# Block-local attention ahead of two routed expert layers: a narrower mask, block maxima taken in another order, nine tiles transposed by a DMA queue, and a new table of priorities

## The chip, the cores and the metric

The kernel runs on one core of one Trainium2 chip. The metric is the device time of one execution in microseconds (us). The engines are named as the profile names them: PE (TensorE; PEld is its weight load), DVE (VectorE), ACT (ScalarE), POOL (GpSimd) and SP (the engine that only issues DMAs here).

## What is computed

The reference is an attention over 4 batches of 8 heads, 768 positions of 64 elements, followed by two expert layers over the 3072 resulting rows. Only the attention, and the gate scores of the first expert layer that close it, are touched by the change.

```python
block, window = (32, 16)
k_sum = k.reshape(B, H, nb, block, D).max(axis=3)
v_sum = v.reshape(B, H, nb, block, D).mean(axis=3)
scores_l = scale * np.matmul(q, k.transpose(0, 1, 3, 2))
mask_l = np.abs(pos[:, None] - pos[None, :]) < window
scores_s = scale * np.einsum('bhsd,bhnd->bhsn', q, k_sum)
scores_s = scores_s + np.log(block)
scores_l_m = np.where(mask_l, scores_l, -1000000000.0)
scores_all = np.concatenate([scores_l_m, scores_s], axis=-1)
a = np.exp(scores_all - np.max(scores_all, axis=-1, keepdims=True))
a = a / (np.sum(a, axis=-1, keepdims=True) + 1e-09)
return np.matmul(a, np.concatenate([v, v_sum], axis=2))
...
logits = x @ w_gate
```

Each query sees the keys less than 16 positions away, and one summary key for each of 24 blocks of 32 positions: the elementwise maximum of the block's keys. The first expert layer then assigns all 3072 rows to 8 experts of 384 places by sorted scores, so nothing of it can begin before the last row's scores are there.

## The kernel before

**Tiling.** The attention works on 8 groups, a batch and 4 heads each (`d['n']` 0 to 7; two groups make a batch). A group is prepared by `prep` and then computed in 6 units of 128 queries (`unit`, c = 0 to 5). Positions are laid out so that one partition holds two neighbouring positions, r = 0 and 1. Numbers are carried as a float16 high part and a float16 low part (the rest), so most steps stand twice.

**Preparation of a group.** `split_qk` makes high and low parts of k and q in three chunks (ACT line 175; the subtraction at line 168 on POOL, for group 0 on DVE). `tr_k` and `tr_q` transpose them on PE (lines 192, 202, 213) into PSUM, and DVE (line 183) and ACT (line 184) copy them out. `kmax` makes the summary keys: PE transposes the float32 keys, 4 heads in each of 3 chunks (line 225, 12 matmuls), DVE reduces each chunk to maxima over 16 columns (line 227), ACT and DVE split the result (lines 229, 230), PE brings the two halves of the partitions together with a constant matrix (line 235), DVE takes the larger (lines 238, 239), and ACT and DVE split again into `ksT` (lines 240, 241). `values` splits v, sums it over blocks on PE, and lays it out in the tile `W` by 13 DMAs (lines 257, 269).

**A unit.** PE writes the mask into a PSUM bank by a matmul with an identity (line 293, 4 x 120 columns: for each head 96 local columns and 24 summary columns), adds the summary scores (line 296) and the local scores (line 302). DVE takes the row maximum (line 308), ACT the exponential (line 312), PE transposes the result (line 317), ACT and DVE split it (lines 320, 321), PE multiplies it with `W` into `po` (line 332), DVE divides (lines 334 to 336) into `xt`. After a batch's second group the rows of a unit are complete: one of 24 tiles `ti`. ACT and POOL split it into `xs` (lines 340, 341), SP writes it to the scratch tensor `xscr` (line 342), PE transposes it in 8 matmuls (line 345), ACT and DVE copy 4 of them each into `xT` (lines 184 and 183), PE computes the gate scores (lines 384, 385), ACT and DVE add them up into `L` (lines 351, 352).

**What sets the order.** Each operation is recorded with an engine, a planned duration, the tiles that it reads and writes and a priority. `Sched.order` replays them: every engine takes, among the operations whose inputs are ready in that replay, the one with the smallest priority, and each engine's instructions are then emitted in that order and run in it on the chip, whatever the real durations are. The priority is the group's and unit's number plus an entry of the table `BIAS1`, looked up by engine and tile name (a `p` ahead of the name is group 0's preparation, a `z` the last group's units). The constants of the routing stages are recorded with priority 60 through a helper whose line is 395. The expert stages have a planner of their own, with a table `BIAS2`, and follow the attention in every engine's stream.

**Buffers that matter.** The tiles `xs` exist 4 times, `xT`, `kn`, `ksT` and `W` twice. All DMAs of the attention are issued by SP, in one order; an SP instruction that waits holds all behind it.

Of the kernel before, what the change touches and what calls it, by code (L numbers as in the profile page):

```python
# [133 lines left out]
class Att:  # L134
# [51 lines left out]
    def tr_k(self, d, c, i, eng, P):  # L186
        nc=self.nc; s=d['ksp',c]; kT=d['kT']; rd=[s.name+'l',s.name+'h']
        if i==0:
            ms,tp=self.half()
            def f():  # L190
                for h in range(4):
                    for r in range(2): nc.tensor.transpose(tp[:,h,r],s[:,h,r].rearrange("p a d -> p (a d)"),self.C['idh'])
            self.pe(.45,rd,[ms.name],f,P)
            self.evac(eng,kT[:,i,:,:,8+128*c:136+128*c],tp,[ms.name],[(kT.name,i,c)],P)
            return
# [10 lines left out]
    def tr_q(self, d, c, eng, P):  # L206
# [7 lines left out]
        self.pe(.45,[s.name+'l',s.name+'h'],[ms.name],f,P)  # L214
        self.evac(eng,qT[:,:,256*c:256*c+256],tp.rearrange("p h r j -> p h (r j)"),[ms.name],[(qT.name,c)],P)

    def kmax(self, d, P):

        nc=self.nc; t=self.wk.tile; kn=d['kn']; V=nc.vector
        kp=t([128,4,24],F32,"kp"); ph,pl=t([128,96],F16,"kph"),t([128,96],F16,"kpl"); km=t([128,96],F32,"km"); ksT=d['ksT']=t([128,2,4,24],F16,"ksT")  # L220

        for c in range(3):
            ms=self.ps.tile([128,512],F32,"ms"); m3=ms.rearrange("p (h j) -> p h j",h=4)
            def f(c=c,m3=m3):
                for h in range(4): nc.tensor.transpose(m3[:,h],kn[:,c,h].rearrange("p r d -> p (r d)"),self.C['idf'])
            self.pe(.47,[(kn.name,c)],[ms.name],f,P)
            self.dve(512,[ms.name],[(kp.name,c)],lambda c=c,m3=m3: V.reduce_max(kp[:,:,8*c:8*c+8],m3.rearrange("p h (n j) -> p h n j",j=16),axis=AX.X),P)
        kk=[(kp.name,c) for c in range(3)]; kf=kp.rearrange("p h n -> p (h n)")
        self.act(96,kk,[ph.name],lambda: nc.scalar.activation(ph,kf,AF.Copy),P)
        self.dve(96,kk+[ph.name],[pl.name],lambda: V.tensor_sub(pl,kf,ph),P)  # L230

        ms=self.ps.tile([128,512],F32,"ms")
        def f():
            for r in range(2):
                for i,x in enumerate((ph,pl)): nc.tensor.matmul(ms[:,96*r:96*r+96],self.C['dup'][:,r],x,start=(i==0),stop=(i==1),skip_group_check=True)
        self.pe(.2,[ph.name,pl.name],[ms.name],f,P)
        o=[ksT[:,i].rearrange("p h n -> p (h n)") for i in range(2)]
        self.dve(96,[ms.name],[km.name],lambda: V.tensor_copy(km,ms[:,:96]),P)
        self.dve(96,[ms.name,km.name],[km.name],lambda: V.tensor_max(km,ms[:,96:192],km),P)
        self.act(96,[km.name],[(ksT.name,0)],lambda: nc.scalar.activation(o[0],km,AF.Copy),P)  # L240
        self.dve(96,[km.name,(ksT.name,0)],[ksT.name],lambda: V.tensor_sub(o[1],km,o[0]),P)

    def values(self, d, P):
# [9 lines left out]
        for i in (0,1,2,3,4,7):  # L253

            lo,hi,j,c0,c1,w=(max(0,32*i-8),min(128,32*i+40),max(0,8-32*i),0,3,slice(i,12,4)) if i<4 else (120,128,0,0,2,slice(4,12,4)) if i==4 else (0,8,40,1,3,slice(3,8,4))
            for r in range(2):
                self.dma((hi-lo)*(c1-c0)*1660,vk+['kpads'],([('We',n,r,i)] if i>3 else [])+[(W.name,r,i)],lambda lo=lo,hi=hi,p=48*r+j,c0=c0,c1=c1,w=w,r=r: nc.sync.dma_start(W[p:p+hi-lo,w],vs[lo:hi,c0:c1,r]),P)
# [11 lines left out]
        self.dma(478000,[vw.name+'h',vw.name+'l'],[(W.name,2)],lambda: nc.sync.dma_start(W[96:120],vw[:,None,:].to_broadcast([24,12,516])),P)  # L269
# [16 lines left out]
    def unit(self, d, c, T):  # L286
# [5 lines left out]
        def f():  # L292
            nc.tensor.matmul(sc,C['idb'],m[:,None,:].to_broadcast([128,4,120]),start=True,stop=False,skip_group_check=True)
# [11 lines left out]
        self.pe(.95,rd,[sn],f,T)  # L305
# [31 lines left out]
        if g==1:  # L337
# [5 lines left out]
            ms,_=self.half(); x8=ms.bitcast(F16).rearrange("p (i j) -> p i j",i=8)  # L343
            def f4():
                for i in range(8): nc.tensor.transpose(x8[:,i],xf[:,128*i:128*i+128],C['idh'])
            self.pe(.45,[xs.name+'h',xs.name+'l'],[ms.name],f4,T)
            self.evac('A',xT[:,:4],x8[:,:4],[ms.name],[xT.name+'h'],T,512)
            self.evac('D',xT[:,4:],x8[:,4:],[ms.name],[xT.name+'l'],T,512)
# [550 lines left out]
class Moe2(Ops):  # L899
# [73 lines left out]
BIAS1={'ACT L': 15.48, 'ACT a': 648.82, 'ACT ah': -1.09, 'ACT kT': -68.21, 'ACT kph': 36.51, 'ACT ksT': 18.87, 'ACT ksp': -8.93, 'ACT pkT': -5.63,   # L973
    'ACT pkph': -46.46, 'ACT pksT': 31.69, 'ACT pksp': 1.25, 'ACT pqsp': 43.19, 'ACT pvm': 72.68, 'ACT pvs': 9.61, 'ACT qsp': 11.16, 
    'ACT vm': -120.37, 'ACT vs': 49.68, 'ACT xT': 81.6, 'ACT xs': -53.13, 'ACT zL': 19.69, 'ACT za': -25.1, 'ACT zah': -84.77, 'ACT zxs': -41.97, 
    'DVE L': -4.27, 'DVE al': 631.85, 'DVE kT': -2.83, 'DVE km': 3.54, 'DVE kp': -22.03, 'DVE kpl': -22.43, 'DVE ksT': -0.4, 'DVE nb': 2.43, 
    'DVE need': -71.59, 'DVE pkT': -3.3, 'DVE pkm': 1.04, 'DVE pkp': -53.59, 'DVE pkpl': 4.91, 'DVE pksT': 33.61, 'DVE pksp': -14.27, 
    'DVE pqT': 120.54, 'DVE pqsp': -12.12, 'DVE pvs': -74.64, 'DVE qT': -80.69, 'DVE rc': -61.0, 'DVE rs': 0.4, 'DVE sc': 150.33, 
    'DVE xT': -19.42, 'DVE xt': 157.4, 'DVE zL': 73.4, 'DVE zcmp': -4.41, 'DVE zm': 31.67, 'DVE znb': -223.07, 'DVE zoh': 2.32, 
# [107 lines left out]
```

## Time and profile before

| | us |
|---|---|
| runs shown (3) | 820.58, 824.24, 826.77; median 824.24 |
| the profiled execution | 827.03 |
| its span, first to last instruction | 825.3 |

The profile's busy times are, of the span: PE 708.4 us (86%), DVE 631.1 (76%), ACT 411.8 (50%), POOL 225.9 (27%). In the trace a time such as 198.33 is counted from the span's start. The attention takes the first 228 us of the span or so; the routing of the first expert follows at once. An operation's duration in a row of the trace runs until its end is reported, so the durations of neighbours on one engine overlap a little: DVE's row maximum lasts 0.66 us, and the next instruction can start 0.57 us after it.

### The profile page before, as it was taken

What the parts mean: (1) busy time and instruction counts of PE and PEld (TensorE: products, weight loads), DVE (VectorE), ACT (ScalarE), POOL (GpSimd) and SP (SyncE); (2) the same over time, 40 slices, a digit from 0 to 9 for tenths busy, and PEclk for the clock granted to TensorE, in tenths of its full rate; (3) what the DMA queues carried; (4) which work ended last, traced back from release to release, by engine and by line L of the source; (5) the groups of instructions that cost most, each with busy time, mean ns of one, the idle gap of its engine ahead of it and who ended that gap; (6) DMA issues with size and microseconds to landing.
All of it is one profiled execution on the core that took longest, in us unless ns stands there. A gap on an engine that the chain in (4) does not pass through costs nothing. (4 is left out here: it accounts for less than half of the span.)

```text
span 825.3 us, 22067 instructions
## 1 busy us (share of the span) xinstructions
PE 708.4 (86%) x8531; PEld 483.7 (59%) x8531; DVE 631.1 (76%) x1900; ACT 411.8 (50%) x794; POOL 225.9 (27%) x233
## 2 busy tenths in 40 slices
PE   3879899898834988999989899699899998999793
PEld 2768778787633545554545454355567657775671
DVE  7999789788777788989889888666469675755750
ACT  3778889685702352525252526443444454646330
POOL 2775664631301011111111113011112222221210
PEclk9999999899955998999999999999999999999897
DMA  7686886432206095869786969999996898799810
GB/s 221 172 224 178 250 214 192 116 96 73 79 13 230 2 275 114 248 146 308 124 282 135 292 157 302 259 278 341 243 260 115 308 361 214 253 327 278 284 31 6
DMA packets 163171, 165.03 MB, mean 200 GB/s; under 512 B 75734, under 2 KB 123862, under 8 KB 163057
## 3 DMA queue, kind: packets, MB, share of 16 engines
q1 hardware_dynamic: 155184, 141.47, 62.0%
q0 software_dynamic: 7872, 22.05, 8.2%
q8 instruction: 69, 1.13, 0.6%
q14 instruction: 46, 0.37, 0.1%
HBM read 114.35 MB, written 29.91 MB: 175 GB/s over the span
## 5 line engine op out<-in xcount | busy, mean ns | idle before, releaser
L708 PE MATMUL ph<-xT,w1h 128*128 128x384 f16 x512 | 102.3, 339 | 12.7 <-DVE hl L712 7.0
L951 PE MATMUL ph<-xT,w1h 128*128 128x128 f16 x1152 | 90.7, 223 | 11.5 <-DVE hl L955 7.4
L951 PEld LDWEIGHTS <-w1h 128*128 128x128 f16 x1152 | 73.6, 100 | 16.1 <-issue 12.4
L722 PE MATMUL py<-w2h,hh 128*128 128x512 f16 x192 | 74.0, 385 | 5.6 <-ACT yt L726 5.6
L684 POOL DMA_INDIRECT xg<-xscr,idx x24 | 30.6, 1273 | 168.6 <-DVE idx L607 64.9
L708 PEld LDWEIGHTS <-w1h 128*128 128x128 f16 x512 | 47.8, 101 | 46.5 <-issue 20.4
L711 ACT ACTIVATE hh<-ph 128x384 f16<-128x384 f32 x64 | 31.3, 489 | 85.9 <-PE ph L708 71.0
L722 PE MATMUL py<-w2l,hh 128*128 128x512 f16 x192 | 74.0, 385 | 0.0
L722 PE MATMUL py<-w2h,hl 128*128 128x512 f16 x192 | 73.8, 384 | 0.0
L645 POOL DMA_INDIRECT out<-xg,oid x18 | 30.4, 1691 | 128.9 <-DVE xg L966 74.2
L925 DVE SCALAR_TENSOR_TENSOR w1l<-wst,w1h 128x1024 f16<-128x1024 f32 x44 | 52.1, 1221 | 10.2 <-ACT w1h L924 9.2
L672 ACT ACTIVATE w1h<-wst 128x1024 f16<-128x1024 f32 x32 | 33.5, 1054 | 51.0 <-DMA wst<-moe_w 50.9
L954 ACT ACTIVATE hh<-ph 128x512 f16<-128x512 f32 x36 | 21.4, 593 | 74.5 <-PE ph L951 71.9
L951 PE MATMUL ph<-xT,w1l 128*128 128x128 f16 x576 | 57.3, 223 | 0.1
L925 DVE SCALAR_TENSOR_TENSOR w2l<-wst,w2h 128x1024 f16<-128x1024 f32 x44 | 52.8, 1220 | 5.5 <-ACT w2h L924 3.7
L962 PE MATMUL py<-w2h,hl 128*128 128x512 f16 x144 | 54.6, 379 | 2.6 <-DVE hl L955 2.5
L645 POOL DMA_INDIRECT out<-yt,dni x24 | 28.0, 1167 | 104.1 <-DVE dw L757 63.4
L722 PEld LDWEIGHTS <-hh 128*128 128x128 f16 x384 | 33.8, 101 | 37.1 <-issue 8.8
L312 ACT ACTIVATE a<-sc,nb 128x120 f32<-128x120 f32 x192 | 53.8, 377 | 3.4 <-DVE nb L310 3.3
L962 PE MATMUL py<-w2h,hh 128*128 128x512 f16 x144 | 54.6, 379 | 0.0
L962 PE MATMUL py<-w2l,hh 128*128 128x512 f16 x144 | 54.6, 379 | 0.0
L924 ACT ACTIVATE w2h<-wst 128x1024 f16<-128x1024 f32 x44 | 45.6, 1052 | 17.4 <-DMA wst<-moe_w 7.1
(348 smaller groups left out, 1845.6 us busy)
## 6 DMA issues: line engine op xcount, KB each, us to landing
wst<-moe_w SPq DMA_DIRECT2D x152, 512.0 KB
ysc<-yt SPq DMA_DIRECT2D x8, 1539.0 KB
kn<-k SPq DMA_DIRECT2D x24, 256.0 KB
qn<-q SPq DMA_DIRECT2D x24, 256.0 KB
vn<-v SPq DMA_DIRECT2D x24, 256.0 KB
xscr<-xs SPq DMA_DIRECT2D x24, 256.0 KB
W<-vs SPq DMA_DIRECT2D x32, 145.1 KB
W<-vs SPq DMA_DIRECT2D x32, 120.9 KB
```

What stands on the lines that cost most here:

```text
L312: for h in range(4): nc.scalar.activation(a[:,h],sc[:,h],AF.Exp,bias=nb[:,h:h+1],scale=0.125)
L645: s=self.nc.gpsimd.indirect_dma_start(out=self.out,out_offset=bass.IndirectOffsetOnAxis(ap=idx,axis=0),in_=x,in_offset=None,bounds_check=3 ...
L672: self.act(1080,[st.name],[hk],lambda st=st,h=h: nc.scalar.activation(h,st,AF.Copy,scale=32.),P)
L684: self.s.op('POOL',1.1,[idx.name]+[('xscr',c) for c in range(24)],[xg.name],lambda xb=xb,i=i: nc.gpsimd.indirect_dma_start(out=xb,out_offs ...
L708: nc.tensor.matmul(ph[:,:384],a[:,kc,fs],b[:,kc],start=(n==0),stop=(n==11))
L711: self.act(384,[ph.name],[(hh.name,fb)],lambda ph=ph,fb=fb: nc.scalar.activation(hh[:,fb],ph[:,:384],AF.Relu),P+.1)
L722: nc.tensor.matmul(py,a[:,fb,sl],b[:,fb],start=(n==0),stop=(n==23))
L924: self.act(1080,[st.name],[hk],lambda st=st,h=h: nc.scalar.activation(h,st,AF.Copy,scale=16.),P-.2)
L925: self.dve(1024,[st.name,hk],[lk,(lk,0),(lk,1)],lambda st=st,h=h,l=l: V.scalar_tensor_tensor(l,st,16.,h,op0=ALU.mult,op1=ALU.subtract),P-.2)
L951: nc.tensor.matmul(ph[:,128*fi:128*fi+128],w[:,kc,fs],x[:,kc],start=(n==0),stop=(n==11)); n+=1
L954: self.act(512,[ph.name],[(hk,q)]+before(H,q),lambda p4=p4,o=o: nc.scalar.activation(o,p4,AF.Relu),P)
L962: nc.tensor.matmul(py,x[:,fb],w[:,fb],start=(n==0),stop=(n==23))
```

## The change

The mask's matmul covers the 96 local columns of each head alone. In `kmax` DVE first takes the larger of the two neighbouring positions for all three chunks in one instruction (`kx`, 128 x 768 float32, both inputs in SBUF), PE transposes half as many columns (6 matmuls in two PSUM tiles), DVE reduces them in two instructions, ACT and DVE split 48 columns, four matmuls with the constant matrix fill 192 columns, and one DVE copy makes `ksT`. Tiles 12 to 20 are no longer transposed by PE: SP issues a DMA transpose from `xs` to `xT`, which also takes their two copies from ACT and DVE. Some planned durations are changed, and the table `BIAS1` is replaced.

```diff
-        kp=t([128,4,24],F32,"kp"); ph,pl=...; km=t([128,96],F32,"km"); ksT=...
-        for c in range(3):
-            ms=self.ps.tile([128,512],F32,"ms"); m3=ms.rearrange("p (h j) -> p h j",h=4)
-            def f(c=c,m3=m3):
-                for h in range(4): nc.tensor.transpose(m3[:,h],kn[:,c,h].rearrange("p r d -> p (r d)"),self.C['idf'])
-            self.pe(.47,[(kn.name,c)],[ms.name],f,P)
-            self.dve(512,[ms.name],[(kp.name,c)],lambda c=c,m3=m3: V.reduce_max(kp[:,:,8*c:8*c+8],...),P)
...
-        self.dve(96,[ms.name],[km.name],lambda: V.tensor_copy(km,ms[:,:96]),P)
-        self.dve(96,[ms.name,km.name],[km.name],lambda: V.tensor_max(km,ms[:,96:192],km),P)
-        self.act(96,[km.name],[(ksT.name,0)],lambda: nc.scalar.activation(o[0],km,AF.Copy),P)
-        self.dve(96,[km.name,(ksT.name,0)],[ksT.name],lambda: V.tensor_sub(o[1],km,o[0]),P)
+        kx=t([128,3,4,64],F32,"kx",bufs=1); km=t([128,2,24],F32,"km"); kh,kl=t([128,48],F16,"kmh"),t([128,48],F16,"kml"); ksT=...
+        self.dve(1150,[(kn.name,c) for c in range(3)],[kx.name],lambda: V.tensor_max(kx,kn[:,:,:,0],kn[:,:,:,1]),P)
+        for g in range(2):
+            ms=self.ps.tile([128,512],F32,"ms")
+            def f(g=g,ms=ms):
+                for c in range(3): nc.tensor.transpose(ms[:,128*c:128*c+128],kx[:,c,2*g:2*g+2].rearrange("p h d -> p (h d)"),self.C['idf'])
+            self.pe(.4,[kx.name],[ms.name],f,P)
+            self.dve(384,[ms.name],[(km.name,g)],lambda g=g,ms=ms: V.reduce_max(km[:,g],ms[:,:384].rearrange("p (n j) -> p n j",j=16),axis=AX.X),P)
+        self.act(60,kk,[kh.name],lambda: nc.scalar.activation(kh,kf,AF.Copy),P)
+        self.dve(500,kk+[kh.name],[kl.name],lambda: V.tensor_sub(kl,kf,kh),P)
...
+                for e in range(2): nc.tensor.matmul(m4[:,i,:,e],self.C['dup'][:,e],x.rearrange("p (g n) -> p g n",g=2),start=True,stop=True,skip_group_check=True)
+        self.dve(192,[ms.name],[ksT.name],lambda: V.tensor_copy(ksT.rearrange("p i h n -> p (i h n)"),ms[:,:192]),P)
...
-            nc.tensor.matmul(sc,C['idb'],m[:,None,:].to_broadcast([128,4,120]),start=True,stop=False,skip_group_check=True)
+            nc.tensor.matmul(sc[:,:,:96],C['idb'],m[:,None,:96].to_broadcast([128,4,96]),start=True,stop=False,skip_group_check=True)
...
+            if 12<=ti<21:
+                self.dma(650000,[xs.name+'h',xs.name+'l'],[xT.name+'h',xT.name+'l'],lambda: nc.sync.dma_start(xT,xf,transpose=True),T,1.4)
+            else:
...
-BIAS1={'ACT L': 15.48, 'ACT a': 648.82, 'ACT ah': -1.09, 'ACT kT': -68.21, 'ACT kph': 36.51, 'ACT ksT': 18.87, 'ACT ksp': -8.93, 'ACT pkT': -5.63, 
+BIAS1={'ACT L': -2.88, 'ACT a': 60.67, 'ACT ah': 2.66, 'ACT kT': 59.22, 'ACT kmh': -59.63, 'ACT ksp': -3.15, 'ACT pkT': -2.19, 'ACT pkmh': 15.8, 
...
```

The lines of the code behind line 221 move up by four with the change, so that the same statement has a smaller number there.

How the new table and costs move instructions is shown at three places. The first is DVE's stream where the routing stages' constants are made (line 395; `sg`, `l96a`, `l96g`, `l96` and `g32` are such constants; `qT0`, `kT0` are tiles of the preparation, `al`, `xt`, `rs` of the units). Before, they stand between units 0 to 3 of group 0:

```order
L395 TENSOR_SCALAR sg_150<-sgf_149 128x4x9
L334 TENSOR_SCALAR rs0_216<-po0_232 128x4
L310 TENSOR_SCALAR nb0_214<-sc0_210 128x4
L395 SCALAR_TENSOR_TENSOR sg_150<-sgf_149,sg_150 128x4x9
L335 RECIPROCAL rs0_216<-rs0_216 128x4
L321 TENSOR_TENSOR al1_223<-pa1_219,ah1_221 120x512
L183 COPY kT0_178<-ms2_177 128x8x128
L336 TENSOR_TENSOR xt0_224<-po0_232,rs0_216 128x256
L395 TENSOR_SCALAR l96a_152<-l96i_151 96x192
```

With the change they stand among units 3 to 5 of group 5 and the first units of group 6 (`xt6` and `xt7` are the rows of group 5's units 3 and 4, `L_122` the gate scores):

```order
L332 TENSOR_TENSOR xt6_229<-po0_231,rs0_215 128x256
L304 TENSOR_REDUCE sc0_209<-sc0_209 128x4
L352 TENSOR_TENSOR L_122<-L_122,ms2_177 128x8
L395 TENSOR_SCALAR sg_150<-sgf_149 128x4x9
L306 TENSOR_SCALAR nb0_213<-sc0_209 128x4
L330 TENSOR_SCALAR rs1_216<-po0_231 128x4
L395 SCALAR_TENSOR_TENSOR sg_150<-sgf_149,sg_150 128x4x9
L331 RECIPROCAL rs1_216<-rs1_216 128x4
L317 TENSOR_TENSOR al0_221<-pa0_217,ah0_219 120x512
L332 TENSOR_TENSOR xt7_230<-po0_231,rs1_216 128x256
```

All nine of these constants' instructions have moved there from group 0, where preparation of the next group stood around them.

The second place is SP's stream, behind the loads for group 6, where the rows of group 5 (tiles 12 to 17, in `xs0` to `xs3` by turns) go out. Before, they are plain writes to `xscr`, with the DMAs into group 7's `W1` between them:

```order
L269 DMA W0_180<-vw0_184 24x12x516
L342 DMA xscr_125<-xs0_233 128x1024
L342 DMA xscr_125<-xs1_234 128x1024
L342 DMA xscr_125<-xs2_235 128x1024
L257 DMA W1_181<-vs1_183 40x3x516
L342 DMA xscr_125<-xs3_236 128x1024
```

With the change:

```order
L341 DMA_TRANSPOSE xT0_236<-xs0_232 128x8x128
L338 DMA xscr_125<-xs0_232 128x1024
L395 DMA sgf_149<-moe2_w_gate 128x4x8
L341 DMA_TRANSPOSE xT1_237<-xs1_233 128x8x128
L338 DMA xscr_125<-xs1_233 128x1024
L265 DMA W0_180<-vw0_184 24x12x516
L341 DMA_TRANSPOSE xT0_236<-xs2_234 128x8x128
L253 DMA W1_181<-vs1_183 40x3x516 x2
L341 DMA_TRANSPOSE xT1_237<-xs3_235 128x8x128
L253 DMA W1_181<-vs1_183 48x3x516
```

Each tile now has a transpose ahead of its write, into `xT0` and `xT1` by turns, and the DMA that completes group 6's `W0` stands behind two of them.

The third place is PE's stream at the end of the attention: the products `po` of group 7's units 3, 4 and 5 (line 332, with the change 328), the gate scores (line 384) and the transposes (line 345). Each row is the first of its operation. Before:

```order
L332 MATMUL po0_232<-W1_181,ah1_221 64x65
...
L384 MATMUL ms0_175<-wg_119,xT0_237 128x16
...
L345 MATMUL ms1_176<-idh_63,xs3_236 128x128
...
L332 MATMUL po0_232<-W1_181,ah0_220 64x65
...
L345 MATMUL ms0_175<-idh_63,xs0_233 128x128
...
L384 MATMUL ms2_177<-wg_119,xT1_238 128x16
...
L332 MATMUL po0_232<-W1_181,ah1_221 64x65
```

With the change, from the transposed exponentials of unit 5 on:

```order
L313 MATMUL pa1_218<-idf_58,a1_212 120x128
...
L384 MATMUL ms0_175<-wg_119,xT0_236 128x16
...
L328 MATMUL po0_231<-W1_181,ah0_219 64x65
...
L384 MATMUL ms1_176<-wg_119,xT1_237 128x16
...
L345 MATMUL ms0_175<-idh_63,xs1_233 128x128
...
L328 MATMUL po0_231<-W1_181,ah1_220 64x65
...
L384 MATMUL ms1_176<-wg_119,xT1_237 128x16
```

The scores of tile 18, whose `xT0` now comes by the queue, stand ahead of unit 4's product, and those of tile 19 ahead of unit 5's. In the last row the engine is at tile 20 or 21, and the transposes of tiles 22 and 23 stand behind both.

## Rows read from the trace of the kernel before

**Rows 1.** Busy time by stretch: from:to, length, each engine's busy us (xinstructions), PEclk, DMA share, GB/s

```profile
25.00:60.00 35.00, 28.46 (x586) 23.78 (x581) 33.52 (x72) 29.78 (x74) 26.73 (x36) 1.00 0.77 198
60.00:125.00 65.00, 59.99 (x1316) 50.09 (x1314) 55.89 (x163) 56.92 (x152) 41.60 (x41) 0.97 0.79 216
125.00:198.00 73.00, 68.67 (x1467) 58.57 (x1467) 62.77 (x177) 60.91 (x168) 32.55 (x31) 0.95 0.44 125
198.00:228.00 30.00, 24.44 (x497) 20.06 (x495) 21.52 (x73) 17.65 (x51) 7.98 (x8) 0.87 0.20 65
```

**Rows 2.** The same view of line 395 alone (the constants): busy us of DVE, of POOL

```profile
41.00:58.00 17.00, 8.03 (x9) 1.38 (x6) 1.00 0.83 211
```

**Rows 3.** Timeline of DVE and POOL, 49 to 53 us: start us, us, engine, line, operation

```profile
49.90 2.23 POOL L251 TENSOR_TENSOR vs<-vn,vs 128x512 f16<-128x512 f32 x2 [1.82 <-ACT vs L175]
51.23 1.01 DVE L395 TENSOR_SCALAR l96g<-l96i 96x192 f32<-96x192 int32 x1
52.20 1.16 POOL L168 TENSOR_TENSOR qsp<-qn,qsp 128x512 f16<-128x512 f32 x1
52.33 1.25 DVE L395 SCALAR_TENSOR_TENSOR l<-l96a,l96g 96x192 f16<-96x192 int32 x1
```

**Rows 4.** Groups by line, first 230 us: operation xcount | busy us, mean ns | idle before

```profile
L345 PE MATMUL ms<-idh,xs 128*128 128x128 f16 x192 | 15.2, 222 | 0.9 <-POOL xs L341 0.6 <-DVE L L352 0.2
L184 ACT ACTIVATE xT<-ms 128x512 f16<-128x512 f16 x24 | 14.6, 608 | 3.2 <-DVE xT L183 1.3 <-DVE L L352 0.8 <-PE ms L345 0.7
L183 DVE COPY xT<-ms 128x512 f16<-128x512 f16 x24 | 10.1, 420 | 4.0 <-ACT xT L184 2.2 <-PE ms L345 1.4
L227 DVE TENSOR_REDUCE kp<-ms 128x32 f32<-128x512 f32 x24 | 15.5, 685 | 6.0 <-PE ms L225 6.0
L293 PE MATMUL sc<-mm,idb 128*128 128x480 bf16 x32 | 12.5, 389 | 0.9 <-ACT a L312 0.9
L296 PE MATMUL sc<-ksT,qT 128*128 128x24 f16 x384 | 17.6, 174 | 1.0 <-DVE ksT L241 0.8
L230 DVE TENSOR_TENSOR kpl<-kp,kph 128x96 f16<-128x96 f32 x8 | 5.6, 702 | 0.5 <-ACT kph L229 0.3
L241 DVE TENSOR_TENSOR ksT<-km,ksT 128x96 f16<-128x96 f32 x8 | 3.8, 476 | 0.1
```

**Rows 5.** Lines 230 and 168 on DVE: duration ns min/median/max, first and last start

```profile
L230 DVE TENSOR_TENSOR kpl<-kp,kph x8: 248/258/2915, 21.8 to 201.3; 128x96 f16<-128x96 f32 x8
L168 DVE TENSOR_TENSOR ksp<-kn,ksp x3: 681/682/682, 10.1 to 15.9; 128x512 f16<-128x512 f32 x3
```

**Rows 6.** Timeline of the last group's summary keys, 198 to 203 us

```profile
198.33 1.53 PE L225 MATMUL ms<-idf,kn 128*128 128x128 f32 x12
199.09 1.89 DVE L227 TENSOR_REDUCE kp<-ms 128x32 f32<-128x512 f32 x3 [1.06 <-PE ms L225]
202.86 0.26 DVE L241 TENSOR_TENSOR ksT<-km,ksT 128x96 f16<-128x96 f32 x1
```

**Rows 7.** Timeline, four stretches: DMA transposes of the first expert layer, and PE waiting

```profile
346.44 1.38 SPq L736 DMA_TRANSPOSE yT<-yt  x1
351.88 0.18 PE L384 MATMUL px<-sg,yT 128*128 128x18 f16 x1 [1.29 <-DMA yT<-yt]
...
509.62 1.28 SPq L736 DMA_TRANSPOSE yT<-yt  x1
517.46 0.18 PE L384 MATMUL px<-sg,yT 128*128 128x18 f16 x1 [0.58 <-DMA yT<-yt]
```

**Rows 8.** Timeline of the attention's end

```profile
217.04 1.16 POOL L341 TENSOR_TENSOR xs<-xt,xs 128x512 f16<-128x512 f32 x1 [2.35 <-ACT xs L340]
...
220.86 0.25 PE L332 MATMUL po<-W,ah 120*64 120x65 f16 x4 [0.29 <-DVE xt L336]
...
226.83 0.18 ACT L351 ACTIVATE L<-ms 128x8 f32<-128x8 f32 x1 [0.88 <-PE ms L385]
```

**Rows 9.** The view of rows 1 for line 293 alone (a unit's mask), group 6's six units

```profile
172.00:188.00 16.00, 2.19 (x6) 0.59 (x6) 1.00 0.43 132
```

More of the change, by code (lines that the diff above doesn't have):

```diff
@@ L237, in kmax @@
-        o=[ksT[:,i].rearrange("p h n -> p (h n)") for i in range(2)]
-        self.dve(96,[ms.name],[km.name],lambda: V.tensor_copy(km,ms[:,:96]),P)
-        self.dve(96,[ms.name,km.name],[km.name],lambda: V.tensor_max(km,ms[:,96:192],km),P)
-        self.act(96,[km.name],[(ksT.name,0)],lambda: nc.scalar.activation(o[0],km,AF.Copy),P)
-        self.dve(96,[km.name,(ksT.name,0)],[ksT.name],lambda: V.tensor_sub(o[1],km,o[0]),P)
+        kx=t([128,3,4,64],F32,"kx",bufs=1); km=t([128,2,24],F32,"km"); kh,kl=t([128,48],F16,"kmh"),t([128,48],F16,"kml"); ksT=d['ksT']=t([128,2,4,24],F16,"ksT")
@@ new lines, in kmax @@
+        kk=[(km.name,0),(km.name,1)]; kf=km.rearrange("p g n -> p (g n)")
+        self.act(60,kk,[kh.name],lambda: nc.scalar.activation(kh,kf,AF.Copy),P)
+        self.dve(500,kk+[kh.name],[kl.name],lambda: V.tensor_sub(kl,kf,kh),P)
+        ms=self.ps.tile([128,512],F32,"ms"); m4=ms[:,:192].rearrange("p (i g e n) -> p i g e n",i=2,g=2,e=2)
+        def f():
+            for i,x in enumerate((kh,kl)):
+                for e in range(2): nc.tensor.matmul(m4[:,i,:,e],self.C['dup'][:,e],x.rearrange("p (g n) -> p g n",g=2),start=True,stop=True,skip_group_check=True)
@@ L342, in unit, with f4 @@
             self.dma(296000,[xs.name+'h',xs.name+'l'],[('xscr',ti)],lambda: nc.sync.dma_start(self.xscr[128*ti:128*ti+128],xf),T)
[L343 to L348, printed above, removed]
+            if 12<=ti<21:
+                self.dma(650000,[xs.name+'h',xs.name+'l'],[xT.name+'h',xT.name+'l'],lambda: nc.sync.dma_start(xT,xf,transpose=True),T,1.4)
+            else:
+                ms,_=self.half(); x8=ms.bitcast(F16).rearrange("p (i j) -> p i j",i=8)
+                def f4():
+                    for i in range(8): nc.tensor.transpose(x8[:,i],xf[:,128*i:128*i+128],C['idh'])
+                self.pe(.5,[xs.name+'h',xs.name+'l'],[ms.name],f4,T)
+                self.evac('A',xT[:,:4],x8[:,:4],[ms.name],[xT.name+'h'],T,512)
+                self.evac('D',xT[:,4:],x8[:,4:],[ms.name],[xT.name+'l'],T,512)
             pl=self.ps.tile([128,512],F32,"ms")
@@ L970, in slot @@
         self.s.op('POOL',1.1,[yg.name,yg.name+"o",oid.name],[('out2',G,a)],f,P,dma=.73)
-BIAS1={'ACT L': 15.48, 'ACT a': 648.82, 'ACT ah': -1.09, 'ACT kT': -68.21, 'ACT kph': 36.51, 'ACT ksT': 18.87, 'ACT ksp': -8.93, 'ACT pkT': -5.63,
[L974 to L979, printed above, removed]
-    'DVE zrs': -12.21, 'DVE zsc': 3.75, 'DVE zw': -8.57, 'DVE zwm': 58.4, 'DVE zxT': 72.43, 'DVE zxt': -3.46, 'PE ms': -732.6, 'PE pa': 2.3,
-    'PE pms': -0.16, 'PE po': -88.64, 'PE sc': -0.26, 'PE zms': -7.05, 'PE zpa': 129.27, 'PE zpo': -87.37, 'PE zsc': -1.66, 'POOL ksp': 49.23,
-    'POOL pkpads': 1.8, 'POOL pvw': -12.97, 'POOL qsp': 232.24, 'POOL rc': -9.83, 'POOL vs': -2.17, 'POOL vw': -1.42, 'POOL xs': -41.19,
-    'POOL zxs': 3.57, 'SP W': 1.24, 'SP We': 12.8, 'SP kn': 109.59, 'SP pW': 2.0, 'SP pWe': 166.12, 'SP pkn': -13.1, 'SP pqn': 39.4,
-    'SP pvn': 60.42, 'SP qn': 434.29, 'SP rc': 22.42, 'SP vn': 434.97, 'SP xscr': -225.41, 'SP zxscr': 12.31}
```

31 lines of the change are left out of this document (17 added, 14 removed).

## The prediction

> **What bounds the kernel now.** I read first the busy time by stretch, since the change touches only the attention, then the groups of instructions by line, for the price of each operation, then the timeline where an engine is full or where a chain stands alone, and last the DMA transposes of the later stages, the only ones that this trace has.
>
> In the stretch from 25 to 60 us DVE is the bound: 33.52 of 35 us, against 28.46 on PE and 29.78 on ACT [rows 1]. From 60 to 198 us no engine is alone: PE 128.7 of 138 us, DVE 118.7, ACT 117.8, summed over the two stretches [rows 1]. PE is nearest, but a unit passes through PE, DVE, ACT and back several times, so an instruction taken from one of the three gives back only part of its time. From 198 us on only the last group's units are left, PE falls to 24.44 of 30 us [rows 1], and what counts is the chain through each unit, which ends with the last gate scores at 226.83 [rows 8]. Routing follows and cannot start earlier; nothing behind it is edited, so a microsecond taken from the attention is taken from the kernel.
>
> **The change part by part.**
>
> *The constants leave group 0.* Nine instructions of line 395 hold DVE for 8.03 us between 41 and 58 us [rows 2], where it is full. Most of that is standing still: 51.23 l96g lasts 1.01 us and ends just as POOL's subtractions of 49.90 end (52.13), and the next, started at 52.33, lasts 1.25 us and ends 0.2 us behind POOL's instruction of 52.20 [rows 3]. Nothing of this work is saved, it is moved to group 5 and 6, where DVE is busy 62.77 of 73 us and POOL 32.55 instead of 26.73 of 35 [rows 1]. There I charge 2 us for them.
>
> What the stretch gains is bounded by the next engine: ACT's 29.78 of 35 us leaves 5.2 us. On the other side some early constants, which stood ahead of the first row maximum, now stand behind it. That lets the units begin some microseconds earlier and loads group 0 by the same amount, so I count nothing for it. I take 6 us gained less the 2 us charged: **−4 us**, from −7 to 0.
>
> *The summary keys.* PE: the 12 transposes of a group take 1.53 us in a row [rows 6], so six fewer save 0.77 us in each of 8 groups, 6.1 us; the matmuls with `dup` shrink from 96 to 48 columns, worth nothing that a row shows. DVE before: three reductions at 0.685, `kpl` 0.702, `ksT` 0.476 [rows 4], and two further instructions on 96 columns that I put at 0.26 each, like the undisturbed `ksT` of 202.86 [rows 6]: 3.75 us. After: `kx` is not in this trace. The nearest row has the same form, two SBUF inputs and 512 columns, at 0.682 us [rows 5], so 768 columns come to 1.02 us, and it can be held up as `kpl` is: 0.702 on average against 0.248 at best, 2.915 at worst [rows 4, 5]. I take the average stall, 0.45: 1.47. Two reductions of 384 columns at three quarters of 0.685 make 1.03, `kml` like `kpl` 0.70, the copy of 192 columns 0.35 by a line between 96 columns (0.26) and 512 (0.42 [rows 4]). Sum 3.55 us: DVE gains 0.2 us a group, 1.6 us in all, and with `kx` at the worst stall each time it would lose 18 us. ACT loses one of two small instructions.
>
> The row shows that DVE waits for POOL here, not what POOL pays. The Trainium skill (page "SBUF — State Buffer", section "SBUF: two separate sides") says that a DVE instruction with two SBUF inputs and a GpSimd instruction that reads SBUF exclude each other for the whole instruction, whichever starts first. That speaks against `kx`: by it, eight instructions of 1.02 us would also hold POOL for 8.2 us in all. The trace agrees on DVE's side, by the 1.25 us just named; POOL stands idle long enough between its pieces of work that the sum would be the same.
>
> *The mask.* 480 columns take 389 ns and 24 take 174 [rows 4]: 0.47 ns a column, so 96 fewer save 45 ns in 48 units, 2.2 us of PE.
>
> *Nine tiles by the queue.* PE is rid of 9 x 0.63 us (15.2 us over 24 tiles), 5.7 us; ACT of 9 x 0.608, 5.5 us; DVE of 9 x 0.42, 3.8 us [rows 4]. Six of the nine tiles lie before 198 us.
>
> *What the less work is worth.* Between 60 and 198 us the sums are, for 6 groups of summary keys, 36 units and 6 tiles: PE 4.6 + 1.6 + 3.8 = 10.0 us, DVE 1.2 + 2.5 = 3.7, ACT 3.6 and a little. The least of these is what all three give, the largest what PE alone would. I take a value nearer to the small end: **−5 us**, from −1 to −10.
>
> *The last summary keys.* At 198.33 the chain from the transposes to the finished `ksT` (202.86 + 0.26) takes 4.8 us [rows 6], and units of the last group wait for it. The new order keeps it there, but the DVE part shrinks from 1.89 us of reductions to about 1.0 us, and three short steps at its end (copy, maximum, split, with an ACT step between) become one: **−1.6 us**, from −2.5 to +1 if `kml` meets a POOL instruction.
>
> *Waiting for the queue.* A DMA transpose of the same size was issued at 346.44 and PE, which stood waiting, had it at 351.88: 5.4 us. Another, with weight loads around it, took from 509.62 to 517.46, 7.8 us [rows 7]. Each also holds SP for 1.3 us, nine times; W's DMAs and the row writes queue behind. PE runs in order, so where a tile is late, everything behind it stands. In groups 5 and 6 a tile's scores follow its rows at a distance of several units, and I charge **+1 us** (0 to +4). At the end the distance is short. Tile 19's rows are complete at 217.04 + 1.16 = 218.2, with 5 us of queue they are there at 223.2, and the scores, which now precede unit 5's product, held at 220.86 before [rows 8], push it back by some 2.5 us. Tile 20 reuses the buffer of tile 18 and so starts only when that was read, and PE's transposes of tiles 22 and 23 stand behind it. DVE and ACT are freed of three tiles' copies there, which buys little in a chain. **+2.5 us**, from 0 to +4.
>
> On this the Trainium skill (page "Advanced Engine Details and Errata", section "X-Bar Transpose (TRN2)") says that transposing DMAs are as fast as plain ones on this chip. No row here has the landing of a plain write to compare; if it held for the landing too, the two waits would stay and the sum with them, since it goes by the 5.4 us that the rows show.
>
> **Sum.** −4 − 5 − 1.6 + 1 + 2.5 = −7.1 us against the profiled execution's 827.03: 819.9. That execution lies 2.8 us above the median of the runs shown (824.24), so against the median I expect **817 us**, 0.9% less.
>
> **Rivals.**
>
> *More than that (812 us or less).* If the three engines are coupled loosely enough that PE, as the busiest, counts alone in the middle, its 10 us come through, and the freed stretch of group 0 gives its whole 7 us: −10 − 7 + 2 (constants) − 1.6 + 2 of waits is −14.6, so 809.6 against the median. For it: PE's 93% in the middle. Against: DVE and ACT at 86% are close behind.
>
> *Nothing to measure (around 824).* The gain of the middle falls to the least, 1 us, because `kx` and the moved constants hit POOL more than I charge, and the waits cost 4 us more: −4 − 1 − 1.6 + 7 is 0. For it: every new DVE instruction with SBUF inputs is of the kind that stood still before.
>
> *Slower: the queue paces group 6 (834 us).* The tiles 12 to 17 share two `xT` buffers, and each transpose waits until the scores two tiles back have read its buffer. If one takes 7.8 us here, as it did at 509.62, and stands behind its neighbour's 1.3 us of issue [rows 7], two tiles need 9.1 us and six 27 us. Group 6's six units, which run beside them, take 16 us now, 2.7 each [rows 9]. PE, in order, then loses 11 us in place of the 1 us charged; the end loses 7.5 in place of 2.5, 2.4 for the tiles 18 and 19 together and as much for tile 20 behind them; and of the middle's gain only the part ahead of group 6 is left, 3 of 5. So −4 − 3 − 1.6 + 11 + 7.5 is +9.9 on 824.2. It decides from the point where a landing takes longer than two units, 5.4 us. Against it: the other landing seen is 5.4 us, and the DMA engines are busy to 0.43 in that stretch [rows 9].
>
> That the change does not do what it says is hardly possible, except for the order: the table moves instructions by planned, not real, durations.
>
> **How the numbers follow.** A measurement of this kernel tells about 1% from no change, that is below 816 or above 832.5 us. The forecast gets 0.42, its own range 812 to 822; more than that 0.22; nothing 0.24; slower 0.12. Of the forecast's weight half lies below 816: faster by over 1% 0.22 + 0.21 = 0.43, within 1% 0.21 + 0.24 less a little that spills over at the upper end, 0.44, slower 0.13. The range that should hold 8 times in 10 reaches from 807 to 828: the whole of the larger gain but its tail, and no change, but not the paced queue.
>
> **What would show it.** Right: in the stretch up to 60 us DVE no longer full, the row maxima of group 0 earlier, and line 395 found at 140 to 180 us; the transposes of line 226 at 0.8 us a group; `kx` between 1.0 and 2.2 us; waits of PE for DMA at line 384 of a few microseconds, most of them for the tiles 18 to 20; the last gate scores near 220 us. Wrong: `kx` near its worst stall, waits of PE for the queue of more than 8 us in all, DVE as full between 25 and 60 us as now, or a last score after 226 us.

## The result and the profile after

The changed kernel takes 811.67 us (median of 6 runs, 809.19 to 815.12), the kernel before 822.41 us beside it (819.51 to 828.41): a ratio of the means of 0.9863, with a 95% interval of 0.9815 to 0.9911, which is 1.4% faster. The forecast was 817.0 us, so the gain was 10.7 us where 7.1 were expected. The two profiled executions, 827.03 and 810.57 us, lie further apart than the medians; the sums below therefore use the attention's own clock, the start of the last gate score, and not the span.

That point moved from 226.83 [rows 8] to 216.91 us, 9.9 us earlier, by one profile of each. The busy time by stretch of the changed kernel, with the columns of [rows 1]:

```profile
25.00:60.00 35.00, 31.66 (x669) 27.45 (x669) 30.41 (x77) 31.10 (x81) 29.09 (x33) 0.95 0.68 184
60.00:125.00 65.00, 61.67 (x1438) 52.74 (x1437) 57.18 (x161) 61.14 (x170) 42.79 (x40) 1.00 0.78 215
125.00:198.00 73.00, 63.16 (x1273) 51.92 (x1274) 61.87 (x172) 50.60 (x139) 34.05 (x38) 0.91 0.69 157
198.00:228.00 30.00, 18.25 (x396) 15.14 (x395) 21.18 (x83) 12.37 (x36) 6.89 (x6) 0.71 0.29 81
```

DVE is no longer full between 25 and 60 us (30.41 of 35 us, 33.52 before), and PE and ACT do more there, 31.66 and 31.10 us. The third stretch is emptier because the attention is ahead of its old times there. The constants, line 395, are found where the new order puts them (the view of [rows 2], two stretches):

```profile
41.00:58.00 17.00, 0.16 (x1) 0.00 (x0) 0.94 0.59 155
140.00:200.00 60.00, 6.65 (x10) 1.21 (x6) 0.89 0.61 121
```

The new instructions of the summary keys, with their durations (ns, min/median/max), first and last start:

```profile
L222 DVE TENSOR_TENSOR kx<-kn x8: 922/954/1773, 11.1 to 154.4; 128x768 f32<-128x768 f32 x8
...
L228 DVE TENSOR_REDUCE km<-ms x16: 537/554/559, 14.4 to 190.3; 128x24 f32<-128x384 f32 x16
...
L231 DVE TENSOR_TENSOR kml<-km,kmh x8: 176/206/3310, 16.0 to 191.2; 128x48 f16<-128x48 f32 x8
```

`kx` takes 0.95 us at the median (1.17 on average), and its last start is at 154.4, while the transposes that read the last one run from 188.79: it is made 34 us ahead of need. The timeline of the last group's keys, the counterpart of [rows 6]:

```profile
188.79 0.50 PE L226 MATMUL ms<-idf,kx 128*128 128x128 f32 x3
...
192.17 0.33 DVE L237 CAST ksT<-ms 128x192 f16<-128x192 f32 x1
...
193.40 0.67 DVE L304 TENSOR_REDUCE sc<-sc 128x4 f32<-128x480 f32 x1 [0.57 <-PE sc L298]
```

From the first transpose to the finished `ksT` it is 3.71 us (4.79 before). The queue and the end of the attention, from the timeline of SP, PE, POOL and ACT:

```profile
159.65 1.25 SPq L341 DMA_TRANSPOSE xT<-xs  x1
164.69 0.18 PE L384 MATMUL ms<-wg,xT 128*128 128x16 f16 x1 [2.03 <-DMA xT<-xs]
...
202.16 2.27 POOL L337 TENSOR_TENSOR xs<-xt,xs 128x512 f16<-128x512 f32 x2 [12.17 <-ACT xs L336]
203.35 2.67 SPq L341 DMA_TRANSPOSE xT<-xs  x2
206.07 1.06 SPq L338 DMA_DIRECT2D xscr<-xs  x2
207.04 0.17 PE L384 MATMUL ms<-wg,xT 128*128 128x16 f16 x1
...
208.53 1.25 SPq L341 DMA_TRANSPOSE xT<-xs  x1
208.97 0.18 PE L384 MATMUL ms<-wg,xT 128*128 128x16 f16 x1
...
211.94 0.17 PE L384 MATMUL ms<-wg,xT 128*128 128x16 f16 x1
...
216.91 0.18 ACT L351 ACTIVATE L<-ms 128x8 f32<-128x8 f32 x1 [0.73 <-PE ms L385]
```

Only at 164.69, for tile 13, did PE stand waiting for a transpose, 5.0 us after its issue; for the tiles 18 to 20 (the rows of line 384 at 207.04, 208.97 and 211.94) it never did.

To see where the 9.9 us arise, the start of each unit's row maximum on DVE (line 308 before, 304 now) was read from both timelines. The changed kernel is ahead by 6.4 us at the first unit of group 2, 11.8 at group 3, 13.6 at group 5, 14.1 at group 6, 11.4 one unit later, 10.9 at group 7 and 9.4 at the last unit. So it gains early, gains more in the middle, gives back some 3 us at the start of group 6, and about 1.5 us over the last group.

### The profile page after: what moved, and what is told of

It reads as the page before. It is cut to its first block, busy times and chain, and to the rows that moved or that the text cites. A ratio compares the mean times of both kernels' runs of the same rounds, so it can differ in the third digit from the quotient of the medians.

```text
span 808.7 us, 21735 instructions
## 1 busy us (share of the span) xinstructions
PE 698.8 (86%) x8411; PEld 476.8 (59%) x8411; DVE 620.3 (77%) x1875; ACT 402.6 (50%) x777; POOL 229.7 (28%) x233
## 5 line engine op out<-in xcount | busy, mean ns | idle before, releaser
L684 POOL DMA_INDIRECT xg<-xscr,idx x24 | 33.3, 1386 | 164.8 <-DVE idx L607 62.4
L708 PE MATMUL ph<-xT,w1l 128*128 128x384 f16 x256 | 54.6, 338 | 0.0
```

What stands on the lines that cost most here:

```text
L684: self.s.op('POOL',1.1,[idx.name]+[('xscr',c) for c in range(24)],[xg.name],lambda xb=xb,i=i: nc.gpsimd.indirect_dma_start(out=xb,out_offs ...
L708: nc.tensor.matmul(ph[:,:384],a[:,kc,fs],b[:,kc],start=(n==0),stop=(n==11))
```

## The experiments

Twelve runs were made, in three batches of four, each batch on a chip of its own. Two measures are used: the last gate score, which needs one profile, and the ratio of times to the kernel before on that chip. The changed kernel's attention was profiled three times (with the first profile and two runs below): 216.91, 217.77 and 215.43 us, mean 216.70. A term of the attention of about 1 us or less is not resolved by one profile, although the first expectations below still count on less.

**The constants alone, in both orders.** PE and ACT keep their order exactly; only the second half of line 395's work, with what follows it, takes another place in the streams of DVE, POOL and SP:

```diff
-        o,self.start=self.order()
+        o,self.start=self.order(); o=place(self,o)
+PLACE={33: 127.13, 34: 140.38, 35: 143.69, 36: 144.01, ...}
+def place(S,o):
+    if S.bias is BIAS1:
+        for j,x in PLACE.items(): S.start[j]=x
+        o=sorted(o,key=lambda j:(S.start[j],j))
+    return o
```

The numbers are planned starts: those of the changed kernel put into the kernel before, and the other way round.

> The kernel before with one thing changed: the second half of the routing constants (nine DVE instructions of line 395 and the five tiny ones of lines 438 and 439, their seven instructions on POOL and two small loads) stands where the changed kernel has it, behind unit 3 of group 5; PE and ACT keep their order. Theory of the prediction: 6 us come back in group 0, 2 us are paid in groups 5 and 6, so about 4 us less than before (818.5 by the median of 822.4), with the row maximum of unit 2.0 some 6 us earlier and that of unit 7.0 only some 4 us earlier. Rival, the order does it: the constants alone are worth under 1 us, because the 8 us on DVE were hidden beside loads or beside PE, and the 6 us seen in group 0 come from the other new priorities.

> The changed kernel with the same constants put back to their places of before, in group 0; PE and ACT keep the changed order. Theory of the prediction: about 4 us more than the changed kernel (815.7 by the median of 811.7), with the row maximum of unit 2.0 about 6 us later and group 6 without its loss of 3 to 4 us between units 5.1 and 6.1. Rival: no difference within 1 us.

Measured: in the kernel before, moving the constants late changes nothing (ratio 0.9994, 0.9969 to 1.002; last gate score 226.51 us). In the changed kernel, putting them back early costs 5.3 us of the attention (221.99 against 216.70; ratio to before 0.9962, 0.9928 to 0.9995). The first is the rival's number, the second the prediction's or a little more. The busy time of the first, in the stretch that was freed:

```profile
25.00:60.00 35.00, 32.39 (x648) 26.90 (x645) 31.05 (x69) 31.77 (x80) 27.48 (x33) 1.00 0.73 184
```

In the old order PE and ACT rise to 32.39 and 31.77 of 35 us when DVE is freed: unit 2.0 comes 2.9 us earlier, not 6, and of this 2.5 us are paid back when the constants are made in groups 5 and 6 (3.4 us ahead at unit 5.1, 0.9 at 6.2). In the changed order the same move is worth 7.5 us at unit 2.0, and 2.3 us are paid back between units 6.0 and 6.1. These 2.3 us can be read in the changed kernel's timeline of DVE and POOL:

```profile
161.61 2.55 DVE L395 TENSOR_SCALAR sg<-sgf 128x36 f16<-128x36 f32 x1
163.00 1.12 POOL L247 TENSOR_TENSOR vs<-vn,vs 128x512 f16<-128x512 f32 x1
165.31 0.65 DVE L304 TENSOR_REDUCE sc<-sc 128x4 f32<-128x480 f32 x1
```

The constant `sg` takes 0.18 us at 167.33 in the kernel before with late constants. Here it lasts 2.55 us and ends 0.04 us behind the last of four POOL instructions in a row, and the row maximum of unit 6.1 (165.31) stands behind it. PE's wait for tile 13 at 164.69 falls into the same moment but is not what is paid: the kernel with early constants has it too (2.04 us, at 172.03) without the loss. What it costs in this order to have the constants early is seen in the timeline of the second kernel:

```profile
50.80 1.15 POOL L168 TENSOR_TENSOR qsp<-qn,qsp 128x512 f16<-128x512 f32 x1
51.91 0.64 POOL L264 TENSOR_TENSOR vw<-vm,vw 24x256 f16<-24x256 f32 x1
52.53 1.14 POOL L168 TENSOR_TENSOR ksp<-kn,ksp 128x512 f16<-128x512 f32 x1
53.63 0.15 POOL L395 IOTA j<- 128x24 f32 x1
53.75 1.12 POOL L247 TENSOR_TENSOR vs<-vn,vs 128x512 f16<-128x512 f32 x1
...
50.86 4.13 DVE L395 TENSOR_SCALAR l96a<-l96i 96x192 int32<-96x192 int32 x1
...
55.38 0.32 PE L328 MATMUL po<-W,ah 120*64 120x65 f16 x4 [3.83 <-DVE xt L332]
```

In the kernel before this constant took 1.07 us at 50.07, and its like 0.24 us at 45.61; here it lasts 4.13 us: it starts 0.06 us behind the start of a POOL instruction and ends 0.12 us behind the end of the last of five, whose reported times leave no gap. DVE's division stands behind it, and PE waits 3.83 us for that. The Trainium skill (page "SBUF — State Buffer", section "SBUF: two separate sides") describes the port that the two share as a lock that one side holds for a whole instruction. The trace agrees in that DVE's instruction ends only behind one of POOL's; by that rule the lock did not come to DVE between POOL's instructions here either.

**The tiles by the queue.** All tiles by PE again, or the last three:

```diff
-            if 12<=ti<21:
+            if False:
```

```diff
-            if 12<=ti<21:
+            if 12<=ti<18:
```

> The changed kernel with all 24 tiles transposed by PE; the table stays, the planner fits the order to it. Theory of the prediction: the six tiles in the middle cost their share of the less work again, some 2 us (3.8 of PE's 10.0 us, of 5), but the waits for the queue, charged at 3.5 us, go: about 1.5 us less than the changed kernel, 810. Rival, the queue costs next to nothing (PE was seen to wait for it once, 2.0 us): 2 to 6 us more than the changed kernel, 814 to 818.

> The changed kernel with tiles 18 to 20 transposed by PE again, 12 to 17 by the queue. Theory of the prediction: the waits at the end, charged at 2.5 us, go, and little is lost, since the end is a chain: 1 to 2.5 us less than the changed kernel, 809 to 811. Rival, the queue is on time at the end too: the three tiles cost PE 0.63 us and ACT 0.61 us each again, so 0 to 2 us more, 812 to 814.

Measured: without the queue the last gate score is at 218.21 us, 1.5 us later than the changed kernel's mean; with the tiles 18 to 20 on PE it is at 216.02, and in two further profiles of that version (below) at 216.66 and 217.88, mean 216.85, no difference. Without the queue PE also runs in another order, and 1.5 us is hardly outside the scatter. So the queue is worth at most a little in the middle and nothing that can be seen at the end, and its waits there cost nothing that can be seen: by the attention both are nearer the rival than the theory.

The whole times did not follow. Without the queue the ratio is 0.9936 (0.9902 to 0.9969); with tiles 12 to 17 on it 1.001 (0.9974 to 1.0046), so a version whose attention is 10 us shorter than before was no faster than before.

**Does the loss behind the attention last?** The changed kernel unedited, and the second version again, on another chip:

> The changed kernel itself, unedited, timed beside the kernel before on the chip of this batch. The first batch showed that what follows the last gate score takes 592 to 605 us by run (profiles), while the attention in front of it repeats to 0.2 us. Theory A, a microsecond of the attention is a microsecond of the kernel on average, and the rest varies by chance: the last gate score at 216.9 again and a ratio to before of 0.986 to 0.990. Theory B, kernels differ in the later part for a lasting reason: the ratio of the first timing (0.9863) comes back on any chip, and tiles 18 to 20 by PE (below) stay near 1.00.

> The kernel with tiles 18 to 20 transposed by PE once more, beside the changed kernel. Its attention ended 0.9 us earlier than the changed kernel's, but its whole time was that of the kernel before (ratio 1.001). Theory A (chance or the chip): a ratio within 0.5% of the changed kernel's in this batch. Theory B (a lasting loss behind the attention): about 1.00 again, some 1.2% over the changed kernel, with more waits of PE at lines 708, 384 and 951.

Measured: the changed kernel 0.989 (0.9849 to 0.9931), the other 1.0007 (0.9978 to 1.0035). The attention did not repeat to 0.2 us (217.77). Otherwise the result is that of theory B: the gain of the changed kernel comes back on a second chip, and the other loses it again behind the attention. The waits there, in DVE's and PE's lists from 220 to 720 us (waiting and awaited line, us, times, longest), for the changed kernel on the second chip and for the other beside it:

```profile
DVE yt L768 <- DMA ysc<-yt: 16.7, 7, 4.2
...
PE ph L708 <- DVE hl L712: 9.5, 6, 3.1
```

```profile
DVE yt L768 <- DMA ysc<-yt: 20.5, 7, 4.7
...
PE ph L708 <- DVE hl L712: 13.4, 7, 3.6
```

Line 768 writes `yt`, one buffer, and must wait until the first expert layer's output of the expert before has left it for `ysc`; the next step on DVE and PE's next products at line 708 stand behind it. Of the other two lines that the expectation names, PE waits longer at 951 too (7.7 and 11.3 us in these lists), but not at 384 (9.7 and 7.5).

**Is it the turn of the DMAs' semaphores?** Small writes of the gate weights behind the attention shift the count; three of them on the slower version, five on the changed kernel:

```diff
-        with tc.manual_schedule(): S.emit()
+        spare=dp.tile([384,64],F16,name="spare")
+        with tc.manual_schedule():
+            S.emit()
+            for x in range(3): nc.sync.dma_start(spare[128*x:128*x+128],C['wg'].rearrange("p c e -> p (c e)"))
```

> Tiles 18 to 20 by PE, and three small writes of 16 KB to a scratch tensor issued by SP behind the last row write, so that as many DMAs as in the changed kernel precede the expert stages. The two batches so far showed that this kernel without them loses some 11 us behind the last gate score (its profiles and medians on two chips), though every instruction there is the same; only the semaphores that DMAs use by turns, eight of them, are shifted by three places. Theory C, the count of DMAs ahead (and so the place in that turn) sets the loss: the loss goes, and the time is 0.3 to 1 us under the changed kernel's, ratio to before about 0.987. Theory D, the place of the instructions in memory or the moment at which routing starts does: no change, ratio 1.00.

> The changed kernel with five such small writes behind the last row write, which brings the turn of the semaphores to the place that it has with tiles 18 to 20 by PE. Theory C: the last gate score stays at 217 to 218 us, and the time rises by some 10 us, ratio to before about 1.00. Theory D: nothing, ratio 0.987 to 0.990.

Measured: 1.018 (1.0141 to 1.0218) with three writes on the slower version, and 0.9857 (0.9825 to 0.989) with five on the changed kernel. Both contradict theory C: the count that should mend made it worse, and the one that should harm did nothing. Theory D as put there isn't borne out either, since the first did change. In the first batch's terms, span less last gate score, the part behind the attention took 834.4 − 217.88 = 616.5 us against 805.0 − 215.43 = 589.6 us of the other on the same chip. Part of where it went can be read. First the waits of the kernel with five writes:

```profile
DVE yt L768 <- DMA ysc<-yt: 8.8, 7, 1.9
...
PE ph L708 <- DVE hl L712: 5.0, 6, 1.6
```

Then those of the one with three:

```profile
DVE yt L768 <- DMA ysc<-yt: 29.3, 7, 5.8
...
PE ph L708 <- DVE hl L712: 18.4, 6, 5.5
```

The first of these lists varies between profiles of one kernel too: for the changed kernel it comes to 10.8 us in the first profile, 16.7 on the second chip and 8.8 here with the five writes, and to 16.8 in the kernel before. On this chip the write of the same 1539 KB lands later in the slower version. In the timeline of the kernel with five writes, from its issue to DVE's release:

```profile
309.93 0.39 SPq L771 DMA_DIRECT2D ysc<-yt  x1
318.78 0.17 DVE L768 CAST yt<-dtb 128x3 f32<-128x3 int32 x1 [0.58 <-DMA ysc<-yt]
```

and in that of the kernel with three:

```profile
311.24 0.40 SPq L771 DMA_DIRECT2D ysc<-yt  x1
323.42 0.17 DVE L768 CAST yt<-dtb 128x3 f32<-128x3 int32 x1 [3.90 <-DMA ysc<-yt]
```

That is 8.9 and 12.2 us; over the experts 7.8 to 10.4 us in the one and 11.4 to 14.2 us in the other. How much of the 27 us this makes is not shown, and why the same write lands later is open: no run separates the place of tensors, of instructions and the moment at which that stage begins.

**The summary keys and the mask.** The old keys in the changed code (their old table entries with them), and the mask over 480 columns again under exactly the changed order:

```diff
-        kx=t([128,3,4,64],F32,"kx",bufs=1); km=...
+        kp=t([128,4,24],F32,"kp"); ph,pl=...
...
```

```diff
-            nc.tensor.matmul(sc[:,:,:96],C['idb'],m[:,None,:96].to_broadcast([128,4,96]),...)
+            nc.tensor.matmul(sc,C['idb'],m[:,None,:].to_broadcast([128,4,120]),...)
```

> The changed kernel with the summary keys made as before (12 transposes, three reductions, the longer tail), their old entries of the table and everything else as changed. Theory of the prediction: 0.77 us of PE in each group, half of it worth time, and 1.6 us at the last group: the last gate score 4 us later than the changed kernel's 216.9. Rival, the summary keys are made ahead of need everywhere: less than 1 us.

> The changed kernel with the mask's matmul over 4 x 120 columns again; the order is exactly the changed one. Theory of the prediction: 48 times 45 ns is 2.2 us of PE, about half of which is time: the last gate score 1 us later. Rival, PE decides everywhere in the middle: 2 us later; or nowhere: 0.

Measured: the full mask ends at 218.24 us, 1.5 us later; between the two numbers expected, and hardly outside the scatter. The old keys end at 246.07 us (one run, 849.27 us in all), which fits neither theory. The planner, given other operations, makes another order from the same table, so this run says more of the order than of the keys. They were tried the other way, in the old order:

```diff
...
+            def g(c=c,ms=ms):
+                if c==0: V.tensor_max(kp,kn[:,:,:,0],kn[:,:,:,1])
+                else: V.reduce_max(km[:,c-1],ms[:,:384].rearrange("p (n j) -> p n j",j=16),axis=AX.X)
...
```

In this kernel (where the pair maximum is called `kp`) the copy to `ksT` may find its PSUM bank already written by a later step, so some summary keys have other values; kinds, sizes and order of the instructions are as described. The other is the changed code under the old table.

> The kernel before with the new summary keys alone, each new instruction in the slot of an old one (the pair maximum in the first reduction's, the copy in the last split's), the rest in the old order but for a few neighbours. Theory of the prediction: half of 0.77 us of PE in each of 8 groups and 1.6 us at the last group: the last gate score 3 to 5 us before 226.7. Rival, the keys are ready ahead of need in all groups but the last: 1 to 2 us. Rival on the other side, the pair maximum stands against POOL and holds DVE: 0 or later.

> The changed code (mask, summary keys, queue, planned durations) under the old table of priorities; names that are new have no entry. Theory of the prediction: all of the gain but the constants' 4 us belongs to the work, so the last gate score comes 5 to 6 us before 226.7. Rival, the table has to fit the code (the old summary keys under the new table ended at 242.2): 230 or later.

Measured: the new keys in the old slots end at 228.74 us, 1.9 us later than before (one profile each); the rival on the other side by its number, although the rows below show mainly PE standing. The new code under the old table ends at 237.13 us (one run, 837.69 us): that rival too. (The expectation names 242.2 for the old keys under the new table; that is the score of an earlier tile, the last one is the 246.07 above.) The groups by line of the first show how the keys lose in a wrong place (operation xcount | busy us, mean ns | idle before it and for what):

```profile
L230 DVE TENSOR_TENSOR kp<-kn 128x768 f32<-128x768 f32 x8 | 10.1, 1264 | 0.0
L226 PE MATMUL ms<-idf,kp 128*128 128x128 f32 x48 | 8.5, 304 | 11.4 <-DVE kp L230 9.3 <-ACT ksp L175 1.3 <-DVE qT L183 0.9
```

PE stands 9.3 us before the transposes, in 7 of 8 groups, because the pair maximum, which they now need, sits where a reduction that follows them used to sit. By the row maxima this kernel is 2.3 us behind at unit 2.0 and 4.1 at 6.5, and then gains 2.2 us over the last group (1.9 behind at 7.5). In the changed kernel nothing on PE waits for `kx`.

## Why the prediction was nearly right, point by point

*The constants (−4 charged).* Right in the changed order, by mechanism and nearly by size: 7.5 us gained early and 2.3 paid late, 5.1 us between the two last scores of the first profiles, where 6 and 2 were charged. What the prediction did not see is that the term belongs to the order: in the old one the move is worth 0.3 us, which one profile each does not tell from nothing. The bound that it named, ACT's spare time, does not explain the difference, and its own 6 us were already more than the 5.2 us that this bound left: between 25 and 60 us PE and ACT end up about as full in either order (32.39 and 31.77, 31.66 and 31.10 of 35 us). What differs is what the constants made PE wait for. Between 41 and 60 us PE stood 5.7 us for DVE with early constants in the changed order, 3.8 of them behind the one long `l96a`, and 0.2 us with late ones; in the old order 4.6 us and none. These waits account for 5.5 of the 7.5 us; why of the 4.6 only 2.9 arrive at unit 2.0 is open, and 2.5 of those are then paid in groups 5 and 6.

*Less work in the middle (−5), the last keys (−1.6) and the waits in groups 5 and 6 (+1).* Together −5.6. The kernel with early constants differs from the one before by all of these and not by the constants' place: it is 1.1 us behind at unit 2.0 and 5.5 ahead at 7.0, behind the last keys, so 6.6 us between. The sum holds to 1 us, in part by luck: −5 was a choice within −1 to −10, what was charged with +1 came as one wait of 2.0 us, and the parts are less close. The last keys' own chain gave 1.1 us, not 1.6: both batches of transposes stay in the chain with a reduction each. The work that PE was to save was read nearly right: up to 230 us its key transposes take 9.0 us (14.5 before), those of the tiles 10.3 (15.2) and the mask 16.6 (18.6). A group's six key transposes take 1.05 us at the last group, not 0.8. The pair maximum costs 1.17 us on average, where 1.47 was charged, and 0.92 without a stall, where 1.02 was. But its price is not what matters: it is made early, where it holds nobody. That the same keys lose some 4 us in the old slots up to the last group shows that the share of PE's saved time that becomes time (half, as charged) is no property of the work. How the 6.6 us divide between less work and new priorities is not settled: each edit was undone alone only for the mask (1.5 us, near the scatter) and the queue (1.5 us).

*The waits at the end (+2.5).* This is the step that failed, in both of the times that it was made of. The first is the distance between a tile's rows and its scores. Tile 19's rows were put at 218.2, as in the trace of before, and its scores had to be there for unit 5's product at 220.86, 2.7 us later [rows 8]. In the new order the second of POOL's two pieces that start at 202.16 completes them at 204.43, and the scores stand at 208.97, 4.5 us later. The second is the landing. The 5 us charged were well read from [rows 7] for the one wait that came, 5.0 us at tile 13. At the end, however, PE had tile 18 without waiting 3.7 us after its issue (203.35 to 207.04) and tile 20 3.4 us after (208.53 to 211.94); with landings of 5.0 us it would have stood for each of the three tiles. Why they land sooner there no run shows; the DMA engines are busy to 0.29 from 198 us on, 0.69 in the stretch before. Of the rule that transposing DMAs are as fast as plain ones (the Trainium skill, page "Advanced Engine Details and Errata", section "X-Bar Transpose (TRN2)") the trace shows only the issue, and that differs: two transposes hold SP for 2.67 us, two plain writes of as many bytes for 1.06. What remains of the loss at the end is 0.6 to 1.0 us between unit 7.0 and the last score, but the version without those transposes loses as much there: 23.7, 24.5 and 23.7 us between these two points in its three profiles, 23.5 in the changed kernel, 22.5 before, and 23.1 in the kernel before with late constants, whose instructions there are those of before. So it isn't the queue's, and much of it is scatter.

*Slips in the sums.* By the line that the prediction names, the copy of 192 columns comes to 0.30 us and not 0.35 (it measured 0.35). The pair maximum at its worst stall each time would have cost 16 us, not 18, once the 1.6 us gained otherwise are counted. The waits of the rival without a gain add up to 7.5 us, not 7, which leaves +0.9. None of these moves the forecast.

*The sum.* −5.09 for the constants, +1.08 − 6.55 for work and order up to unit 7.0, +0.64 for the end make −9.92 us, against −7.1 predicted. About 2 us of the difference are the waits at the end, 1 the constants. In time against the median, the reference run (822.41 here, 824.24 in the runs shown) accounts for another 1.8 of the 5.3 us by which 817.0 was high.

*The rivals.* The number of "more than that" (809.6) came nearest, but not by its mechanism: PE's 10 us did not come through in the middle, which with the last keys gave 6.6; the waits were missing. The queue never paced group 6: the one landing that PE stood for took 5.0 us, under its limit of 5.4, and the wait was 2.03 us. That a microsecond of the attention is one of the kernel held for the changed kernel on two chips (9.9 and 10.7 us by the medians; 9.1 and 9.7), but it is no rule: another version lost some 25 us behind an attention that was 2.4 us longer (837.23 against 810.23 us on one chip).

## What to carry to other kernels

Price a moved instruction in the order in which it will stand, not in the one that it leaves: moving the same constants was worth 0.3 us in one order and 5.1 in the other, and the same pair maximum held PE for 9.3 us in one and not at all in the other. Before charging a wait for a late transfer, shift the moment at which its data are ready and the moment at which they are needed by what the new order does to them, and do not carry a landing from one stage into another: 5.0 us in the middle of the attention, at most 3.7 and 3.4 at its end. And time whole kernels even when a stage is measured well: an unedited stage behind it can take back the gain, and a small list of its waits tells part of where.

## What was not expected of the hardware

- A DVE instruction with a single input in SBUF (`l96a`, 96x192 int32) was held for 4.13 us through five POOL instructions in a row; where POOL left it alone it took 0.24 us. `sg`, 36 columns, was held for 2.55 us through four (0.18 us elsewhere). The prediction had read such stalls of constants off single instructions of POOL, 1.0 to 1.25 us.
- The end of the attention repeats only to about 1 us either way (215.43, 216.91, 217.77 us for the same instructions there).
- The same write from `yt` to `ysc`, 1539 KB, released DVE 8.9 us after its issue in one version and 12.2 us in another, on the same chip and with the same instructions in that stage; the two differ by 27 us behind the attention. How much of that the write makes, and why it lands later, is not known.
